# Linear-attention block plus gated MLP on one core: unbroken gate/up groups, other planner priorities, a ring of five exp tiles and two banks for the down projection

## The chip, the core and the metric

The kernel runs on one core of a Trainium2 chip. The metric is device microseconds of one execution; the median of the timed runs counts. The five engines are called here as the profile calls them: PE (matmul; PEld is its weight load), DVE (vector), ACT (scalar), POOL (GpSimd) and SP, whose queue issues nearly all DMAs.

## The reference

With x of 2048 x 448 in bf16, 16 heads of 28, and F = 1792:

```python
xn = layernorm(x); q, k, v = split(xn @ wqkv)          # per head, 28 wide
pq, pk = q @ w_phi, k @ w_phi
phi(z) = concat(softmax(z), softmax(-z))               # 56 features per head
kv = sum_s phi(pk)^T v;  z = sum_s phi(pk)
h = x + ((phi(pq) @ kv) / (phi(pq) @ z + 1e-6)) @ wo
hn = layernorm(h)
out = h + (sigmoid(hn @ w_gate) * (hn @ w_up)) @ w_down
```

## The kernel before

The 2048 tokens are 16 tiles of 128 (t = 0..15) and four chunks of 512 (c = 0..3). The program is a list of operations in `build`, each with an engine, the keys that it reads and writes, an estimated duration `dur`, for a DMA a landing time `lat`, and a priority `prio`. `Graph.schedule` (L69) is a list scheduler that fixes the order on each engine when the kernel is built: it takes the earliest start that any ready operation could have, and among the ready operations of that engine that could start within `TOL` = 0.12 us of it the one with the highest priority. `emit` (L121) writes one in-order stream per engine, with semaphore waits where an operation depends on another engine. So a stream never changes its order on the chip: an operation that the planner put early holds up all that stands behind it. Keys are ordered by program order, so an operation that writes a PSUM bank comes after all operations listed before it that use that bank.

- **Constants and loads** (L307 to L350): POOL sets zeros, the identity, the mask `maskK` and the padded `kvz`. SP issues x tile 0, the k columns of wqkv, x1, the v columns, x2-3, x4-7, then the rest with `after`.
- **wprep** (L365): W_k times w_phi is made on PE (transposes L375, copies on ACT L380 and DVE L383, products L392, copies L398 and L401), with `warm` matmuls on zeros (L356) in the gaps; later the same for W_q.
- **Layernorm 1** (L409 to L442): per tile `bn_stats` and `bn_aggr` on DVE (L416, L418); per group of tiles ([0], [1], [2,3], [4-7], [8-11], [12-15]) `ve1` on DVE (L425), `pow1` on POOL (L427), `nb1` on DVE (L429); then `xn` on ACT (L435) into one of three slots and a DMA transpose on SP into `xnT` (L439).
- **k, v and the kv sum** (L446 to L480): per tile PE makes pk and v (L451); ACT makes exp(pk) and exp(-pk) (L460, L461) and copies v (L463); DVE sums and inverts (L465, L467); POOL multiplies to phi (L469); PE adds to kv (L477) in banks 6 and 7. `ek`, `ss`, `rs`, `phi` and `v1` all have three slots (`NS`).
- **q side** (L482): 16 operations pq (L485) in banks 4 and 5, each with two exps on ACT (L491, L492).
- **Attention per tile** (L549): num on PE (L558; banks 0 and 1 for tiles 1, 3, 5, banks 6 and 7 for the others), six small DVE operations to `rden` (L567 to L578), o on POOL (L580), a transpose, wo on PE in bank 2 (L590), h on DVE (L593), the second layernorm over ACT (L598), DVE and POOL (L603), hn (L607, L608) and a transpose into `xnT` (L611).
- **Gate/up** (L620): chunk 0 in two halves of 256 tokens, then the chunks of 512. The 448 rows of the weights are three k tiles of 128 and one of 64. For two f blocks of 128 columns: operation `gu` (j = 0, banks 4 and 5, priority 20) runs three gate matmuls, three up matmuls (L632) and then `pair`, two matmuls of 64 rows in the two halves of the array (L637, L638). Operations `gg` and `uu` (j = 1, banks 0 and 1, priority 90) begin with their `pair`, then three gate, three up matmuls. ACT makes the sigmoid (L657), DVE the product (L660) into `hhT[c % 2]`.
- **Down** (L664): 14 matmuls per tile (L670) in parts of 4, 4, 3, 3, in bank 3 except for the last chunk; DVE adds h (L676), SP stores (L678).

Of the kernel before, what the change touches and what calls it, by code (L numbers as in the profile page):

```python
# [6 lines left out]
ALU = mybir.AluOpType  # L7
# [7 lines left out]
class _Op:  # L15
    __slots__ = ("i", "eng", "name", "fn", "dur", "prio", "dma", "lat", "deps", "start", "finish", "pos",
                 "need_inc", "sem", "val", "waits", "known", "nkids")


class Graph:  # L20
# [13 lines left out]
    def op(self, eng, name, fn, r=(), w=(), dur=0.1, prio=0.0, dma=None, lat=0.0, nring=0, after=()):  # L34
        o = _Op()
        o.i, o.eng, o.name, o.fn, o.dur, o.prio, o.dma, o.lat = len(self.ops), eng, name, fn, dur, prio, dma, lat
        o.deps = {}
        o.need_inc, o.sem, o.val = False, None, 0
# [30 lines left out]
    def schedule(self):  # L69
        ops = self.ops  # L70
        kids = [[] for _ in ops]
        nd = [len(o.deps) for o in ops]
        for o in ops:
            for j in o.deps:
                kids[j].append(o.i)
        free = {e: 0.0 for e in ENGINES}
        ready = [o.i for o in ops if nd[o.i] == 0]
# [3 lines left out]
        def est(i):  # L81
            o = ops[i]
            a = avail.get(i)
            if a is None:
                a = 0.0
                for j in o.deps:
                    p = ops[j]
                    if p.dma is not None or p.eng != o.eng:
                        f = p.finish + self.SEM_LAT
                    else:  # L90
                        f = p.start + p.dur
                    a = max(a, f)
                avail[i] = a
            return max(a, free[o.eng])
        while ready:
# [10 lines left out]
            o = ops[i]  # L106
            o.start = e
            free[o.eng] = e + o.dur
            o.finish = e + o.dur + o.lat
            ready.remove(i)  # L110
            order.append(i)
            for c in kids[i]:
                nd[c] -= 1
                if nd[c] == 0:
                    ready.append(c)
# [94 lines left out]
P = 128  # L210
D = 448
# [13 lines left out]
def build(nc, A_x, A_wqkv, A_w_phi, A_wo, B_w_gate, B_w_up, B_w_down, out):  # L225
# [10 lines left out]
    with ExitStack() as es:  # L236
# [13 lines left out]
        nb1 = sb("nb1", [P, NT], f32)  # L250
        sum2 = sb("sum2", [P, NT], f32)
# [72 lines left out]
        op("pool", "kvz0", lambda e: e.memset(kvz[:], 0.0), w=["kvz0", "kvz1"], dur=0.9, prio=50)

        def kvz_ones(e):
            for sg in range(2):
                for gg in range(G):
                    p = e.tensor_copy(kvz[:, sg, gg, :].rearrange("p (h e) -> p h e", e=E)[:, :, E - 1], maskK[:, :, 0])
            return p  # L330
        op("pool", "kvzones", kvz_ones, r=["maskK", "kvz0", "kvz1"], w=["kvz0", "kvz1"], dur=1.2, prio=50)


        def xload(a, b, prio, after=()):
            op("sp", "x%d" % a, lambda e: e.dma_start(x_sb[:, a:b, :], x_t[:, a:b, :]), w=[("x", t) for t in range(a, b)],
               dur=0.5, prio=prio, dma="in", lat=1.8 + (b - a) * 0.45, nring=32,
               after=after)

        def wload(j, name, prio, after=()):
            dma_in(wqkv_sb[:, :, j * D:(j + 1) * D], wqkv_v[:, :, j * D:(j + 1) * D], name, 392, prio, after)  # L340
        xload(0, 1, 100)
        wload(1, "wk", 99)
# [5 lines left out]
        xload(1, 2, 97)  # L348
        wload(2, "wv", 96)
        xload(2, 4, 95)  # L350
# [58 lines left out]
        groups = [[0], [1], [2, 3]] + [list(range(4 * c, 4 * c + 4)) for c in range(1, NCH)]  # L409
# [317 lines left out]
```

## Time and profile before

| | |
|---|---|
| median of 3 runs | 237.48 us (236.17 to 238.86) |
| profiled execution | 238.04 us, span 236.3 us |
| PE busy | 218.5 us (92%), 1371 matmuls |
| DVE, ACT, POOL busy | 141.0, 102.3, 60.2 us |
| mean granted PE clock | 0.986 |
| first gate/up matmul, last down matmul's end | 77.25 us, 233.3 us |

The span is from the first to the last instruction of the profiled execution; its own device time is 1.74 us longer. Matmuls overlap in the pipeline, so PE's busy time holds what it waits for within itself; the spacing of starts tells more than a duration. A releaser named "issue" means that the profile shows no wait.

### The profile page before, as it was taken

Reading aid. Unit: us, or ns where it says so; the run is one execution under the profiler, and the core shown is the slowest. Engines: PE = TensorE matmul, PEld = TensorE weight load, DVE = VectorE, ACT = ScalarE, POOL = GpSimd, SP = SyncE. Lnnn points to the kernel's source line nnn. Section 1 sums busy time; section 2 is a strip of 40 time slices with the busy share of each in tenths; the row PEclk is TensorE's granted clock in tenths of the full one; section 3 lists DMA queues with packets and bytes.
Section 4 is the critical chain, followed back from the end, with each engine's and each line's share of the span. In section 5 each row is a group of like instructions: output and inputs, shape, how many; then the busy total and the mean of one; then the engine's idle time right before and its main releaser. Section 6 shows DMA issues by size and latency. Waiting matters only on the chain.

```text
span 236.3 us, 3654 instructions
## 1 busy us (share of the span) xinstructions
PE 218.5 (92%) x1371; PEld 111.1 (47%) x1383; DVE 141.0 (60%) x364; ACT 102.3 (43%) x208; POOL 60.2 (25%) x78
## 2 busy tenths in 40 slices
PE   7679959899997999999999999998999899999994
PEld 3335636555654566665555444333333333334442
DVE  1796995674898687787878676534233243341222
ACT  2588869777689453433343332422312224240000
POOL 7345874874344123203122132000000000000000
PEclk9999988999999799999999999999999999999999
DMA  6697847966123422122122222110000000000101
GB/s 164 171 230 122 251 110 157 239 133 193 22 44 69 89 44 44 27 67 44 22 47 46 65 45 66 22 22 0 21 22 0 19 19 0 3 19 19 58 32 49
DMA packets 35866, 16.66 MB, mean 70 GB/s; under 512 B 27272, under 2 KB 34952, under 8 KB 35848
## 3 DMA queue, kind: packets, MB, share of 16 engines
q1 hardware_dynamic: 35344, 16.39, 29.2%
q8 instruction: 11, 0.18, 0.3%
q10 hardware_dynamic: 504, 0.03, 0.2%
q14 instruction: 7, 0.06, 0.1%
HBM read 8.28 MB, written 1.84 MB: 43 GB/s over the span
## 4 chain that ended last, share of the span: by engine, by line
PE 72%; DVE 10%; DMA 6%; POOL 4%; ACT 4%; issue 2%; SPq 1%; DVEq 0%; POOLq 0%
PE psum L632 33%; PE psum L670 17%; PE psum L637 7%; PE psum L590 5%; POOL phi L469 4%; PE psum L451 3%; PE psum L558 3%; PE psum L485 3%; DMA x_sb<-in_A_x_dram 2%; DMA xnT<-xn_pad 2%; DVE ss L465 2%; DVE hhT L660 1%; DMA xnT<-hn_pad 1%; DVE st L416 1%; PE psum L477 1%
## 5 line engine op out<-in xcount | busy, mean ns | idle before, releaser
L657 ACT ACTIVATE sg_sb<-psum 128x512 bf16<-128x512 f32 (+1 forms) x70 | 35.8, 511 | 83.0 <-PE psum L638 56.7
L660 DVE TENSOR_TENSOR hhT<-psum,sg_sb 128x512 bf16<-128x512 f32 (+1 forms) x70 | 40.4, 584 | 49.5 <-ACT sg_sb L657 31.9
L632 PE MATMUL psum<-xnT,wg_sb 128*128 128x512 bf16 (+1 forms) x202 | 46.8, 338 | 3.1 <-issue 2.4
L632 PE MATMUL psum<-xnT,wu_sb 128*128 128x512 bf16 (+1 forms) x207 | 47.9, 340 | 0.3
L670 PE MATMUL psum<-wd_sb,hhT 128*128 128x448 bf16 x224 | 46.6, 353 | 0.7 <-DVE x_sb L676 0.7
L670 PEld LDWEIGHTS psum<-wd_sb,hhT 128*128 128x128 bf16 x224 | 20.4, 98 | 21.5 <-DVE x_sb L676 2.8
L469 POOL TENSOR_TENSOR phi<-ek,rs 128x896 bf16<-128x896 bf16 x16 | 27.0, 1698 | 10.9 <-DVE rs L467 10.8
L632 PEld LDWEIGHTS psum<-xnT,wu_sb 128*128 128x128 bf16 x210 | 20.7, 99 | 16.0
L632 PEld LDWEIGHTS psum<-xnT,wg_sb 128*128 128x128 bf16 x210 | 16.5, 98 | 24.6 <-issue 11.0
L580 POOL TENSOR_TENSOR o_pad<-c_sb,rden 128x448 bf16<-128x448 bf16 x16 | 15.0, 937 | 47.5 <-DVE rden L578 39.4
L637 PE MATMUL psum<-xnT,wg_sb 64*128 64x512 bf16 (+1 forms) x70 | 20.7, 344 | 1.0 <-DVE hhT L660 0.9
L676 DVE TENSOR_TENSOR x_sb<-psum,x_sb 128x448 bf16<-128x448 f32 x16 | 10.0, 623 | 19.4 <-PE psum L670 19.2
L465 DVE TENSOR_REDUCE ss<-ek 128x32 f32<-128x896 bf16 x16 | 17.2, 1072 | 6.4 <-ACT ek L461 6.4
L638 PE MATMUL psum<-xnT,wu_sb 64*128 64x512 bf16 (+1 forms) x70 | 20.7, 344 | 0.0
L451 PE MATMUL psum<-Wk,xnT 112*128 112x448 bf16 x64 | 15.4, 367 | 2.1 <-DMA xnT<-xn_pad 1.3
L485 PE MATMUL psum<-xnT,Wq 112*112 112x512 bf16 x64 | 15.9, 380 | 0.0
L590 PE MATMUL psum<-wo_sb,oT 112*128 112x448 bf16 x64 | 15.2, 361 | 0.0
L603 POOL TENSOR_TENSOR rst<-ve,neghalf 128x1 f32<-128x1 f32 x16 | 8.8, 553 | 25.0 <-DVE ve L601 24.9
L451 PE MATMUL psum<-wqkv_sb,xnT 112*128 112x448 bf16 x64 | 14.9, 355 | 0.0
L435 ACT ACTIVATE xn_pad<-x_sb,nb,rst 128x448 bf16<-128x448 bf16 x16 | 11.9, 759 | 6.4 <-DVE nb L429 4.4
L598 ACT ACTIVATE junk<-x_sb,nm 128x448 bf16<-128x448 bf16 x16 | 10.6, 664 | 7.5 <-DVE nm L596 7.5
L477 PE MATMUL psum<-v,phi 128*112 128x116 bf16 x128 | 10.0, 223 | 3.7 <-POOL phi L469 3.3
(69 smaller groups left out, 236.2 us busy)
## 6 DMA issues: line engine op xcount, KB each, us to landing
out_dram<-x_sb SPq DMA_DIRECT2D x16, 112.0 KB, 1.7
wd_sb<-in_B_w_down_dram SPq DMA_DIRECT2D x7, 224.0 KB, 4.4
x_sb<-in_A_x_dram SPq DMA_DIRECT2D x3, 448.0 KB, 4.7
wg_sb<-in_B_w_gate_dram SPq DMA_DIRECT2D x3, 448.0 KB, 3.9
wu_sb<-in_B_w_up_dram SPq DMA_DIRECT2D x3, 448.0 KB, 4.5
wqkv_sb<-in_A_wqkv_dram SPq DMA_DIRECT2D x3, 392.0 KB, 4.1
wo_sb<-in_A_wo_dram SPq DMA_DIRECT2D x1, 392.0 KB, 3.6
xnT<-xn_pad SPq DMA_TRANSPOSE x16, 3.3
```

The costliest lines, as they stand in the source:

```text
L451: p = e.matmul(bk(bank)[:, 0:D], lhsT=xnT[t // 4][:GP, kt, TS(t)], rhs=wap(kt), start=(kt == 0), stop=(kt == KT - 1))
L465: op("dve", "ss%d" % t, lambda e: e.tensor_reduce(ss[:, s, :], ek[:, s, :, :].rearrange("p a (h d) -> p (a h) d", d=DH), AX.X, ALU.add), r ...
L469: op("pool", "phi%d" % t, lambda e: e.tensor_tensor(phi[:, s, :, :].rearrange("p a (h d) -> p (a h) d", d=DH), ek[:, s, :, :].rearrange("p ...
L485: p = e.matmul(bk(b)[:GP, 0:512], lhsT=W2[1][:, kt, gg * GP:(gg + 1) * GP], rhs=xnT[c][:GP, kt, :], start=(kt == 0), stop=(kt == KT - 1))
L580: op("pool", "o%d" % t, lambda e: e.tensor_tensor(o_pad[:, s, :, 0:GP].rearrange("p g (h d) -> p g h d", h=4), c_sb[:, s, :, 0:DH].rearran ...
L590: p = e.matmul(bk(2)[:, 0:D], lhsT=oT[:GP, s, kt, :], rhs=wo_sb[:, kt, :], start=(kt == 0), stop=(kt == KT - 1))
L632: p = e.matmul(bk(b)[:, 0:N], lhsT=w[:, kt, fs], rhs=hb[:, kt, ns], start=(st and kt == 0), stop=(sp and kt == 2))
L637: e.matmul(bk(bg)[:, 0:N], lhsT=wg_sb[0:64, 3, fs], rhs=hb[0:64, 3, ns], start=st, stop=not st)
L638: return e.matmul(bk(bu)[:, 0:N], lhsT=wu_sb[64:P, 3, fs], rhs=hb[64:P, 3, ns], start=st, stop=not st, tile_position=(64, 0))
L657: op("act", "sig%d_%d" % (ci, ff), lambda e: e.activation(sg_sb[:, k, 0:N], bk(bg)[:, 0:N], ACT.Sigmoid), r=[B(bg)] + (["sigtab"] if sgn[0 ...
L660: op("dve", "hh%d_%d" % (ci, ff), lambda e: e.tensor_tensor(hhT[(t0 // 4) % NHH][:, ff, ns], bk(bu)[:, 0:N], sg_sb[:, k, 0:N], ALU.mult), ...
L670: p = e.matmul(bk(b)[:, 0:D], lhsT=hhT[c % NHH][:, ff, TS(t)], rhs=wd_sb[:, ff, :], start=(ff == 0), stop=(ff == FT - 1))
```

## The change

`Graph.op` gets `chain` and `urg`. Operations of one chain are ready together, get one start (the latest of each member's need less its offset in the chain) and are emitted back to back; `urg` widens `TOL` for one operation. `gg` and `uu` become members of the chain of their `gu`, at priority 20. `urg` is 0.45 for o, wo and the second layernorm of tiles 0 and 1. Landing times of the first loads and many `dur` values are set anew. The layernorm groups become [0], [1], [2], [3], [4,5], [6,7], [8-11], [12-15], the statistics' priority rises from 46-t to 52-t, and `nb1` moves to POOL, with a new DVE operation `nm1` (minus the mean) ahead of it. `mask0` to `kvzones` stand after the last `pow1` of tiles 6 and 7. `ek` gets five slots inside `hhT[1]`, and `ss`, `rs`, `v1` get five; `phi` keeps three. Down uses banks 2 and 3 in turn for tiles 4 to 11.

```diff
@@ schedule: est of a chain, and the choice
+                a, off = 0.0, 0.0
+                for m in o.chain:
+                    for j in ops[m].deps:
...
+                        a = max(a, f - off)
+                    off += ops[m].dur
...
-                if ops[i].eng == eng0 and e <= m + self.TOL:
+                if ops[i].eng == eng0 and e <= m + self.TOL + ops[i].urg:
...
+            for m in ops[i].chain:
+                o = ops[m]
+                o.start = e
+                e += o.dur
...
+                order.append(m)
@@ buffers
-        ek = sb("ek", [P, NS, 2, D])
-        ss = sb("ss", [P, NS, 2 * H], f32)
-        rs = sb("rs", [P, NS, 2 * H], f32)
+        NE = 5
+        ek = hhT[1][:].rearrange("p f n -> p (f n)")[:, 0:NE * 2 * D].rearrange("p (s a d) -> p s a d", s=NE, a=2)
+        ss = sb("ss", [P, NE, 2 * H], f32)
+        rs = sb("rs", [P, NE, 2 * H], f32)
...
-        v1 = sb("v1", [P, NS, H, EV])
+        v1 = sb("v1", [P, NE, H, EV])
@@ loads: landing times
-        xload(0, 1, 100)
-        wload(1, "wk", 99)
+        xload(0, 1, 100, lat=2.4)
+        wload(1, "wk", 99, lat=4.6)
...
-        xload(1, 2, 97)
-        wload(2, "wv", 96)
-        xload(2, 4, 95)
+        xload(1, 2, 97, lat=4.2)
+        wload(2, "wv", 96, lat=5.4)
+        xload(2, 4, 95, lat=5.5)
...
-                xload(4, 8, 90)
+                xload(4, 8, 90, lat=7.2)
@@ layernorm 1
-        groups = [[0], [1], [2, 3]] + [list(range(4 * c, 4 * c + 4)) for c in range(1, NCH)]
+        groups = [[0], [1], [2], [3], [4, 5], [6, 7]] + [list(range(4 * c, 4 * c + 4)) for c in range(2, NCH)]
...
-               dur=0.58, prio=46 - t)
+               dur=0.57, prio=52 - t)
...
-            op("dve", "nb1_%d" % a, lambda e: e.scalar_tensor_tensor(
-                out=nb1[:, a:b], in0=mv1[:, a:b, 0], scalar=-1.0, in1=rst1[:, a:b], op0=ALU.mult, op1=ALU.mult),
+            op("dve", "nm1_%d" % a, lambda e: e.tensor_scalar(nm1[:, a:b], mv1[:, a:b, 0], -1.0, None, op0=ALU.mult),
+               r=[("mv1", t) for t in ts], w=[("nm1", gi)], dur=0.15, prio=52.9 - a)
+            op("pool", "nb1_%d" % a, lambda e: e.tensor_tensor(nb1[:, a:b], nm1[:, a:b], rst1[:, a:b], ALU.mult),
+               r=[("nm1", gi), ("rst1", gi)], w=[("nb1", gi)], dur=0.25, prio=70 - a)
@@ constants, now listed after layernorm 1
+        op("pool", "mask0", lambda e: e.memset(maskK[:], 1.0), w=["maskK"], dur=0.3, prio=50, after=[pwi[5]])
...
@@ exp of k: slots
-            s = t % NS
+            s = t % NE
+            sp = t % NS
@@ attention: o, wo, h, nm, sq, ve, pow2, hn get urg=ug
+            ug = 0.45 if t < 2 else 0.0
@@ gate/up
-                op("pe", "gu%d_%d" % (ci, ff), fn, r=hk + wgu_keys, w=[B(bg), B(bu)], dur=1.55 * u, prio=20)
+                gch[0] = op("pe", "gu%d_%d" % (ci, ff), fn, r=hk + wgu_keys, w=[B(bg), B(bu)], dur=1.6 * u, prio=20)
...
-                op("pe", "gg%d_%d" % (ci, ff), fn1, r=hk + wgu_keys, w=[B(bg), B(bu)], dur=0.9 * u, prio=90)
-                op("pe", "uu%d_%d" % (ci, ff), fn2, r=hk + wgu_keys, w=[B(bu)], dur=0.65 * u, prio=90)
+                op("pe", "gg%d_%d" % (ci, ff), fn1, r=hk + wgu_keys, w=[B(bg), B(bu)], dur=0.96 * u, prio=20, chain=gch[0])
+                op("pe", "uu%d_%d" % (ci, ff), fn2, r=hk + wgu_keys, w=[B(bu)], dur=0.65 * u, prio=20, chain=gch[0])
@@ down
-                    down(t, 3, [4, 4, 3, 3], 10)
+                    down(t, 3 if t < 4 else (2, 3)[t % 2], [4, 4, 3, 3], 10)
```

## Rows read from the trace of the kernel before

**Rows 1.** Page, granted PE clock in 40 slices of 5.9 us, in tenths

```profile
PEclk9999988999999799999999999999999999999999
```

**Rows 2.** Windows: length, busy us of PE, PEld, DVE, ACT, POOL, clock, DMA, GB/s

```profile
13.30:53.00 39.70, 34.49 (x270) 20.93 (x270) 31.29 (x60) 31.58 (x65) 27.37 (x18) 0.96 0.76 182
...
77.20:211.70 134.50, 131.19 (x783) 61.76 (x795) 77.87 (x213) 44.77 (x95) 16.67 (x23) 0.99 0.15 33
211.70:233.30 21.60, 21.55 (x111) 10.34 (x109) 5.08 (x9) 0.18 (x1) 0.00 (x0) 1.00 0.11 38
```

**Rows 3.** Timeline, start: W_k's preparation (start us, us, engine, line)

```profile
3.90 0.90 POOL L324 MEMSET kvz<- 112x960 bf16 x1
...
7.38 1.09 POOL L329 CAST kvz<-maskK 112x4 bf16<-112x4 f32 x8
...
8.01 0.63 DVE L416 BATCH_NORM_STATS2 st<-x_sb 128x6 f32<-128x448 bf16 x1 [1.16 <-DMA x_sb<-in_A_x_dram]
8.56 0.67 DVE L383 COPY WkT<-psum 112x448 bf16<-112x448 bf16 x2
...
9.28 1.03 PE L392 MATMUL psum<-Wphi,WkT 112*112 112x112 bf16 x16 [1.42 <-DVE WkT L383]
```

**Rows 4.** Timeline, 27 to 35 us: the layernorm of tiles 8 to 11

```profile
27.06 0.12 DVE L418 BATCH_NORM_AGGREGATE mv<-st 128x2 f32<-128x6 f32 x1
...
28.99 1.70 POOL L469 TENSOR_TENSOR phi<-ek,rs 128x896 bf16<-128x896 bf16 x1
...
29.05 1.65 DVE L429 SCALAR_TENSOR_TENSOR nb<-mv,rst 128x4 f32<-128x4 f32 x1
...
30.74 2.06 ACT L435 ACTIVATE xn_pad<-x_sb,nb,rst 128x448 bf16<-128x448 bf16 x3 [1.76 <-DVE nb L429]
...
34.11 1.70 PE L451 MATMUL psum<-Wk,xnT 112*128 112x448 bf16 x4
```

**Rows 5.** Windows around the two stretches at the lower clock

```profile
33.60:37.10 3.50, 3.40 (x19) 2.21 (x20) 2.23 (x8) 2.47 (x6) 2.00 (x2) 0.56 0.49 100
29.70:33.70 4.00, 1.32 (x19) 0.98 (x17) 3.93 (x9) 2.90 (x5) 3.49 (x3) 0.95 0.37 112
75.30:77.20 1.90, 0.07 (x2) 0.00 (x0) 1.90 (x7) 1.88 (x5) 1.44 (x3) 1.00 0.16 31
...
77.60:81.00 3.40, 3.40 (x18) 1.71 (x16) 1.97 (x6) 1.52 (x3) 0.94 (x1) 0.51 0.42 86
```

**Rows 6.** Timeline, before the first gate/up matmul

```profile
76.43 0.62 ACT L492 ACTIVATE eq<-psum 112x512 bf16<-112x512 f32 x1
...
77.25 0.49 PE L632 MATMUL psum<-xnT,wg_sb 128*128 128x256 bf16 x3 [1.88 <-issue]
```

**Rows 7.** PE's timeline: pairs alone and pairs joined

```profile
110.00 0.38 PE L558 MATMUL psum<-kvz,eq 112*128 112x120 bf16 x4
110.21 0.49 PE L632 MATMUL psum<-xnT,wg_sb 128*128 128x256 bf16 x3
...
113.45 0.37 PE L558 MATMUL psum<-kvz,eq 112*128 112x120 bf16 x4
113.76 0.39 PE L637 MATMUL psum<-xnT,wg_sb 64*128 64x512 bf16 x1
...
114.08 0.82 PE L632 MATMUL psum<-xnT,wg_sb 128*128 128x512 bf16 x3
...
209.89 0.39 PE L637 MATMUL psum<-xnT,wg_sb 64*128 64x512 bf16 x1
...
210.12 0.38 PE L637 MATMUL psum<-xnT,wg_sb 64*128 64x512 bf16 x1
```

**Rows 8.** PE's waits, 59 to 234 us: total us, times, longest

```profile
PE psum L637 <- DVE hhT L660: 0.9, 1, 0.9
PE psum L670 <- DVE x_sb L676: 0.7, 1, 0.7
PE psum L632 <- DVE hhT L660: 0.7, 3, 0.3
```

More of the change, by code (lines that the diff above doesn't have):

```diff
@@ L16 @@
     __slots__ = ("i", "eng", "name", "fn", "dur", "prio", "dma", "lat", "deps", "start", "finish", "pos",
-                 "need_inc", "sem", "val", "waits", "known", "nkids")
+                 "need_inc", "sem", "val", "waits", "known", "chain", "head", "urg")
 class Graph:
@@ L32, in __init__, with op @@
         self.ring = {}
-    def op(self, eng, name, fn, r=(), w=(), dur=0.1, prio=0.0, dma=None, lat=0.0, nring=0, after=()):
+    def op(self, eng, name, fn, r=(), w=(), dur=0.1, prio=0.0, dma=None, lat=0.0, nring=0, after=(), chain=None, urg=0.0):
         o = _Op()
@@ L37, in op @@
         o.deps = {}
+        o.chain, o.head, o.urg = [o.i], o.i, urg
+        if chain is not None:
+            o.head = self.ops[chain].head
+            self.ops[o.head].chain.append(o.i)
         o.need_inc, o.sem, o.val = False, None, 0
@@ L71, in schedule @@
         kids = [[] for _ in ops]
-        nd = [len(o.deps) for o in ops]
+        nd = [0] * len(ops)
         for o in ops:
             for j in o.deps:
-                kids[j].append(o.i)
+                if ops[j].head != o.head:
+                    nd[o.head] += 1
+                    kids[j].append(o.head)
         free = {e: 0.0 for e in ENGINES}
-        ready = [o.i for o in ops if nd[o.i] == 0]
+        ready = [o.i for o in ops if o.head == o.i and nd[o.i] == 0]
         order = []
@@ L84, in est @@
             if a is None:
[L85 to L92, printed above, removed]
+                a, off = 0.0, 0.0
+                for m in o.chain:
+                    for j in ops[m].deps:
+                        p = ops[j]
+                        if p.head == o.head:
+                            continue
+                        if p.dma is not None or p.eng != o.eng:
+                            f = p.finish + self.SEM_LAT
+                        else:
+                            f = p.start + p.dur
+                        a = max(a, f - off)
+                    off += ops[m].dur
                 avail[i] = a
@@ L105, in schedule @@
             _, e, i = best
[L106 to L109, printed above, removed]
             ready.remove(i)
[L111 to L115, printed above, removed]
+            for m in ops[i].chain:
+                o = ops[m]
+                o.start = e
+                e += o.dur
+                free[o.eng] = e
+                o.finish = e + o.lat
+                order.append(m)
+                for c in kids[m]:
+                    nd[c] -= 1
+                    if nd[c] == 0:
+                        ready.append(c)
         assert len(order) == len(ops)
@@ L250, in build @@
         nb1 = sb("nb1", [P, NT], f32)
+        nm1 = sb("nm1", [P, NT], f32)
         sum2 = sb("sum2", [P, NT], f32)
@@ L324, in build, with xload @@
[L324 to L334, printed above, removed]
+        def xload(a, b, prio, after=(), lat=None):
@@ L487, in mm @@
                 return p
-            op("pe", "pq%d_%d" % (c, gg), mm, r=W2q + [("xnT", 4 * c + i) for i in range(4)], w=[B(b)], dur=0.9, prio=prio)
+            op("pe", "pq%d_%d" % (c, gg), mm, r=W2q + [("xnT", 4 * c + i) for i in range(4)], w=[B(b)], dur=0.87, prio=prio)
             def eqf(e):
@@ L509, in build, with kvz_ones @@
                 xi[t] = xnorm(t)
+        op("pool", "mask0", lambda e: e.memset(maskK[:], 1.0), w=["maskK"], dur=0.3, prio=50, after=[pwi[5]])
+        op("pool", "mask1", lambda e: e.affine_select(out=maskK[:], in_=maskK[:], compare_op=ALU.is_ge, fill=0.0, base=0,
+                                                      channel_multiplier=1, pattern=[[-DH, 4], [0, EV]]),
+           r=["maskK"], w=["maskK"], dur=0.35, prio=50)
+        op("pool", "mask2", lambda e: e.affine_select(out=maskK[:], in_=maskK[:], compare_op=ALU.is_ge, fill=0.0,
+                                                      base=DH - 1, channel_multiplier=-1, pattern=[[DH, 4], [0, EV]]),
+           r=["maskK"], w=["maskK"], dur=0.35, prio=50)
+        op("pool", "kvz0", lambda e: e.memset(kvz[:], 0.0), w=["kvz0", "kvz1"], dur=0.9, prio=50)
+        def kvz_ones(e):
+            for sg in range(2):
+                for gg in range(G):
+                    p = e.tensor_copy(kvz[:, sg, gg, :].rearrange("p (h e) -> p h e", e=E)[:, :, E - 1], maskK[:, :, 0])
+            return p
+        op("pool", "kvzones", kvz_ones, r=["maskK", "kvz0", "kvz1"], w=["kvz0", "kvz1"], dur=1.2, prio=50)
         for t in range(NT):
```

62 lines of the change are left out of this document (28 added, 34 removed).

## The prediction

> **What bounds the kernel now.** I read the page first, then the windows, then the timeline where they show holes.
>
> The page gives PE 218.5 us busy of a span of 236.3, so PE is the engine to count. Its clock is full but for two places [rows 1]. The windows split the span [rows 2]. From the first gate/up matmul (77.2) to the last down matmul (233.3) PE is busy 131.19 of 134.50 and 21.55 of 21.60 us: there only PE's own work, its clock and 3.3 us of gaps count. From 13.3 to 53.0, which is from the first exp of k to the last, no engine is full: PE 34.49 of 39.70 (pipelined time, so less in truth), ACT 31.58, DVE 31.29, POOL 27.37. That stage is bound by waits in fixed streams, and its fullest engine other than PE, ACT, has 8.1 us to spare.
>
> Where are the waits? At the start DVE copies WkT at 8.56, behind the statistics of tile 2, which waited 1.16 us for x; PE's products of W_k follow at 9.28 after 1.42 us idle [rows 3]. In the middle, DVE aggregates tile 11 only at 27.06; nb1 of tiles 8 to 11 starts at 29.05 and takes 1.65 us; ACT's xn waits 1.76 us for it and starts at 30.74; the next pk matmuls start at 34.11 [rows 4]. PE is busy 1.32 of the 4.00 us from 29.7 to 33.7, and in the 3.5 us after that it has a mean clock of 0.56, so mostly the lower of its levels, 1.2 instead of 2.4 GHz [rows 5]. Before the first gate/up matmul PE stands idle for 1.88 us [rows 6], and then again runs 3.4 us at 0.51 [rows 5].
>
> In gate/up the cost that the change aims at can be seen in the starts of the pairs [rows 7]. A pair alone that ends a stretch (113.76, next matmul 114.08) takes 0.32 us; a pair followed by a pair (209.89, then 210.12) takes 0.23. That is 0.09 us for leaving the 64-row form. Entering it costs as much again: num's four matmuls at 113.45 are followed by the pair 0.31 us later, while the four at 110.00 are followed by a full-row matmul in 0.21. So each separate stretch of pairs costs some 0.19 us. Of the 35 groups of two f blocks, 21 have their two pairs joined (the last at 209.89), 14 have them apart: gg, at priority 90, ran ahead of gu, or other work came between.
>
> **The change, part by part**, against the profiled execution of 238.04 us.
>
> *Early part.* (a) With the new landing times the planner expects x2-3 late, as it is, and can place the WkT copies ahead of its statistics. They end at 9.23; without the wait of 1.16 and the 0.63 of the statistics they would end some 1.8 us earlier [rows 3]. Gain 0 to 1.8. Next late would be the copies of W2 on ACT and DVE. (b) Statistics at 52-t come before ss and rs of earlier tiles, so tiles 8 to 11 are normalised as soon as their group is complete. The hole is worth 4.00 - 1.32 = 2.7 us of idle PE, plus half of the time at the lower clock, 3.5 x 0.44 = 1.5: 4.2 at most [rows 5]. (c) nb1 on POOL takes DVE's 1.65 us off the path, but nm1 is a new DVE operation of the same small size, six becoming eight groups; no row shows it. Bounds per group: 0.15, which the other small DVE operations take, and 1.65, as nb1 did when phi (28.99, 1.70 us) ran on POOL beside it [rows 4]. I take 0.15, because nm1 needs nothing from POOL and can run while pow1 does. (d) Five exp slots let ACT run two tiles further ahead of phi; without a row that shows ACT held for long, I count this only as what lets (a) and (b) go through. (e) The constants go behind pow1 of tiles 6 and 7: kvz's two steps are 0.90 + 1.09 = 2.0 us of POOL [rows 3], and their priority of 50 puts them ahead of phi. Before, phi had not begun then; now they stand in its stream. Cost 0, if POOL's 39.70 - 27.37 = 12.3 us of slack [rows 2] takes them, to 2.0.
>
> Sum of the gains 1.8 + 4.2 = 6.0. It is limited by ACT's 8.1 us of slack, which no in-order stream uses up; I take half, 3.0, because (c) and (e) pull against it and because PE fills part of the time won by doing num and wo of later tiles less early, which it must then do later. Bounds: -1.5 (both late groups held 1.65 in nm1 and nothing won, PE taking up half) to +6.0.
>
> *Hand-over to gate/up.* `urg` lets the planner keep DVE or PE free up to 0.45 us for tiles 0 and 1. But the first gu also uses bank 4 or 5, which all 16 pq use ahead of it: the last exp of these ended at 76.43 + 0.62 = 77.05, and PE began at 77.25 [rows 6]. So landing the tiles earlier wins nothing unless ACT too is earlier. I take 0 by itself, bounds -1.0 to +1.9 (the idle time), and leave the stretch at half clock where it is, since the same idle time comes before it; if that goes, 3.4 x 0.49 = 1.7 more [rows 5].
>
> *Unbroken groups.* 14 stretches of pairs fewer at 0.19: 2.7 us, on PE's path, nothing beside it. Bounds 2.0 (some starts still held by a bank) to 2.7.
>
> *Stalls in gate/up and down.* PE waited 0.9 us once in front of a lone pair for a product on DVE, and 0.7 in three more such waits; 0.7 once for the last add of a down tile in the single bank [rows 8]. The second bank takes away the last; joined groups alternate their banks evenly and should take the 0.9, but the shorter groups of 256 columns leave DVE and ACT less time for the two products. I take 1.2, bounds 0 to 2.3. Moving gg from priority 90 to 20 also means that num and wo (60-t, 70-t) go first whenever they are ready between groups; they wait behind a whole group when not.
>
> The end (last add and store, 3.0 us after 233.3) stays. Sum: 3.0 + 0 + 2.7 + 1.2 = 6.9, so 238.04 - 6.9 = 231.1. The median shown is 0.56 below the profiled execution, so **230.6 us**.
>
> A page speaks against (c). The Trainium skill, "SBUF — State Buffer", section "Who interferes with whom", says that VectorE and GpSimd share a pair of SBUF ports under an exclusive lock, and that `tensor_scalar`, which nm1 is, may use it. By that rule nm1 would be held as nb1 was; the 1650 ns of nb1, ending within 10 ns of the phi beside it, agree with a lock of that kind. What this would make of the time is the second rival.
>
> **The rivals.**
> 1. *All of it is won.* The early 6.0, both clock dips away (1.7 for the second), 2.7, and 2.3 of stalls: 12.7, so 225.3, less 0.56: 224.8 us. For it: 8.1 us of slack on ACT, and PE busy only 1.32 of 4.00 in the hole. Against it: pq's exps must all be done before gate/up, and ACT has those too.
> 2. *The early gain is given back at POOL and DVE.* nm1 held by phi in both late groups costs 3.3, the constants 2.0, which together eat 5.3 of 6.0; PE keeps 2.7 + 1.2 and some half us: 238.04 - 4.4 - 0.56 = 233.1. For it: the 1.65 of nb1. Against it: nm1 stands directly behind ve1 in program order and a hold there would overlap ve1's.
> 3. *Hardly anything:* early part -1.5, joins 2.0, stalls 0: 237.0.
> 4. *Slower: attention starves behind the groups.* A PE step was at most a half group, two times three matmuls of up to 0.82 and a pair of 0.32, 1.96 us; it is now a whole one, 3.9. A num or wo that just misses waits on average 1 us longer. With three such steps per tile (two nums, wo) and 8 tiles in the chunks with 512 columns, that is 24 us if none of it is hidden. The point from which it decides: 6.9 + 2.4 = 9.3 us unhidden. At half, 12 us, the time is 238.04 - 6.9 + 12 - 0.56 = 242.6. For it: banks 6 and 7 hold one tile's num at a time. Against it: PE's 3.3 us idle in 134.5 [rows 2] show that gate/up and down work was there almost always, and down can fill in.
>
> **How the numbers follow.** Forecast (228.5 to 232.5) 0.45; rival 1 (below 228.5) 0.22; rival 2 (to 235) 0.17; rival 3 0.09; rival 4 0.07. One per cent, 2.4 us, is about what a measurement of this kernel can tell from no change. Faster than 235.1: 0.45 + 0.22 + 0.16 = 0.83; slower than 239.9: 0.06; between: 0.11. The range takes rivals 1 and 2 whole: 224.8 rounds to 224.5, and 236.0 lies past rival 2 by a part of rival 3.
>
> **What would show it.** Right: 35 stretches of pairs, each with two pairs some 0.23 us apart; no PE hole with a half clock behind it near 30 us; the first gate/up matmul at about 74; no PE wait on the add of down. Wrong: nm1 with more than 1 us, ACT's xn waiting for POOL's nb1, phi delayed by L324 and L329, a first gate/up matmul still at 77, or PE idle for several us ahead of chunk 1, 2 or 3 with hn's transposes landing just before.

## The result, and the profile after

The median of the kernel after is 228.65 us (4 runs, 227.87 to 230.17), beside 237.67 us (236.17 to 238.86) of four runs of the kernel before. The ratio is 0.9631, 95% interval 0.9557 to 0.9706: 9.0 us faster. The forecast was 230.6 us, 6.9 us below the median of 237.48 us that was known then.

The profiled execution took 227.87 us with a span of 226.2. Differences below between two medians are differences of their ratios to the kernel before, times 237.67 us; stages are read from the profiled executions. One run of a_pairs_apart (the profiled one, 240.27 us at a mean granted clock of 0.943) and one of a_sigld (229.66 us) were over 1.5% longer than the fastest of their kernel and are left out of the medians and ratios.

The page of the kernel after: busy time of the engines, and the granted clock in 40 slices.

```profile
PE 212.0 (94%) x1372; PEld 109.7 (48%) x1383; DVE 143.3 (63%) x368; ACT 101.7 (45%) x208; POOL 62.3 (28%) x88
...
PEclk9999999999999999999999999999999999999999
```

Neither dip of [rows 1] is there. That is this one execution: the other three show a mean clock of 0.991 to 0.993, so in them some stretch still ran at the lower level. No trace shows where.

The windows of the kernel after (length, busy us of PE, PEld, DVE, ACT, POOL, clock, DMA share, GB/s), for the stages of [rows 2] and three pieces of the early part:

```profile
12.00:48.00 36.00, 33.34 (x276) 20.68 (x275) 32.64 (x66) 31.32 (x64) 31.30 (x35) 1.00 0.95 206
...
22.00:28.00 6.00, 6.00 (x55) 3.77 (x52) 5.79 (x13) 6.00 (x13) 4.91 (x4) 1.00 1.10 189
28.00:34.00 6.00, 5.33 (x40) 3.17 (x40) 5.83 (x11) 5.30 (x12) 5.66 (x5) 1.00 1.11 332
34.00:40.00 6.00, 6.00 (x62) 4.25 (x61) 5.22 (x10) 5.65 (x13) 6.00 (x5) 1.00 1.03 217
...
72.17:223.08 150.91, 148.12 (x895) 72.26 (x903) 86.30 (x227) 45.74 (x97) 17.13 (x24) 1.00 0.15 35
```

For comparison, the last of these windows in the kernel before, from its first gate/up matmul to its last down matmul:

```profile
77.25:233.25 156.00, 152.74 (x893) 72.06 (x904) 82.88 (x220) 44.91 (x95) 16.67 (x23) 0.99 0.14 33
```

So 5.1 us went ahead of the first gate/up matmul (77.25 to 72.17) and another 5.1 behind it (156.0 to 150.9). The hole of [rows 5] is closed. In the stage that bounds the early part POOL is now busy 31.30, ACT 31.32, DVE 32.64 and PE 33.34 of 36.0 us; before, POOL was busy 27.37 of 39.70 us [rows 2]. Almost all of the 5.1 us behind the first gate/up matmul is PE's busy time (152.74 to 148.12), not its idle time (3.3 to 2.8).

The timeline of the kernel after, cut to the steps that the prediction names (start us, us, engine, line; in brackets the wait ahead of it and what ended it):

```profile
3.13 0.90 POOL L518 MEMSET kvz<- 112x960 bf16 x1
...
7.40 0.38 DVE L381 COPY WkT<-psum 112x448 bf16<-112x448 bf16 x1
...
8.70 1.00 PE L390 MATMUL psum<-Wphi,WkT 112*112 112x112 bf16 x16 [0.89 <-DMA Wphi<-in_A_w_phi_dram]
...
16.87 1.08 POOL L523 CAST kvz<-maskK 112x4 bf16<-112x4 f32 x8
...
18.45 1.70 POOL L469 TENSOR_TENSOR phi<-hhT,rs 128x896 bf16<-128x896 bf16 x1 [0.51 <-DVE rs L467]
...
19.10 1.07 DVE L423 TENSOR_SCALAR ve<-mv 128x4 f32<-128x4 f32 x1
...
20.09 0.15 DVE L427 TENSOR_SCALAR nm<-mv 128x4 f32<-128x4 f32 x1
...
20.25 1.01 POOL L425 TENSOR_TENSOR rst<-ve,neghalf 128x4 f32<-128x4 f32 x1
...
22.92 0.78 ACT L434 ACTIVATE xn_pad<-x_sb,nb,rst 128x448 bf16<-128x448 bf16 x1
...
28.54 1.07 DVE L423 TENSOR_SCALAR ve<-mv 128x4 f32<-128x4 f32 x1
...
32.78 14.94 POOL L469 TENSOR_TENSOR phi<-hhT,rs 128x896 bf16<-128x896 bf16 x9
...
72.17 0.49 PE L651 MATMUL psum<-xnT,wg_sb 128*128 128x256 bf16 x3
...
73.23 0.67 ACT L616 ACTIVATE junk<-x_sb,nm 128x448 bf16<-128x448 bf16 x1 [2.80 <-DVE nm L614]
...
74.01 1.28 ACT L676 ACT_TABLE_LOAD   x1
...
74.01 0.28 PE L656 MATMUL psum<-xnT,wg_sb 64*128 64x256 bf16 x1 [0.80 <-DVE den L593]
...
76.20 0.50 PE L651 MATMUL psum<-xnT,wg_sb 128*128 128x256 bf16 x3 [1.15 <-DVE hhT L679]
...
125.97 0.39 PE L656 MATMUL psum<-xnT,wg_sb 64*128 64x512 bf16 x1
126.19 0.38 PE L656 MATMUL psum<-xnT,wg_sb 64*128 64x512 bf16 x1
126.51 0.82 PE L651 MATMUL psum<-xnT,wg_sb 128*128 128x512 bf16 x3
```

Tile 8 is normalised at 22.92 where it was 30.74 [rows 4]. The pair at 126.19 follows 0.22 us behind the first, and the next full-row matmul 0.32 behind the second: one stretch of two pairs. 34 of the 35 groups look so, against 21 before. The one that doesn't is the first: its second pair waits 0.80 us for bank 0, which den of tile 5 still reads.

All waits of PE for a semaphore in the last window, after (total us, times, longest), beside [rows 8]:

```profile
PE psum L651 <- DVE hhT L679: 1.4, 2, 1.1
PE psum L656 <- DVE den L593: 0.8, 1, 0.8
```

The wait on down's add is gone, and the two longest waits now stand in the first group. The 1.1 ends with a product that came late because ACT loaded its table (1.28 us at 74.01) before the first sigmoid. The load itself came late because ACT's stream has an activation of the second layernorm ahead of it, which had waited 2.80 us for DVE (73.23). In the kernel before the same load ran right behind the last exp, 0.2 us ahead of the first gate/up matmul (77.25):

```profile
77.06 1.28 ACT L657 ACT_TABLE_LOAD   x1
```

### The profile page after: what moved, and what is told of

Same layout as the page of the kernel before. It is cut to its first block, busy times and chain, and to the rows that moved or that the text cites. A ratio compares the mean times of both kernels' runs of the same rounds, so it can differ in the third digit from the quotient of the medians.

```text
span 226.2 us, 3686 instructions
## 1 busy us (share of the span) xinstructions
PE 212.0 (94%) x1372; PEld 109.7 (48%) x1383; DVE 143.3 (63%) x368; ACT 101.7 (45%) x208; POOL 62.3 (28%) x88
## 4 chain that ended last, share of the span: by engine, by line
PE 73%; DVE 9%; ACT 7%; DMA 6%; POOL 2%; issue 1%; ACTq 1%; SPq 0%; DVEq 0%; POOLq 0%
PE psum L651 32%; PE psum L689 18%; PE psum L656 7%; DMA xnT<-xn_pad 6%; PE psum L450 5%; PE psum L608 5%; PE psum L485 3%; PE psum L576 2%; DVE hn_pad L625 2%; DVE hhT L679 1%; PE psum L477 1%; DVE ss L465 1%; ACT xn_pad L434 1%; ACT hhT L460 1%; ACT hhT L461 1%
## 5 line engine op out<-in xcount | busy, mean ns | idle before, releaser
L651 PE MATMUL psum<-xnT,wu_sb 128*128 128x512 bf16 (+1 forms) x207 | 47.3, 336 | 0.3
L689 PEld LDWEIGHTS psum<-wd_sb,hhT 128*128 128x128 bf16 x224 | 21.5, 98 | 19.9 <-DVE x_sb L695 0.4
L651 PEld LDWEIGHTS psum<-xnT,wg_sb 128*128 128x128 bf16 x210 | 17.0, 97 | 23.4 <-issue 11.6
L469 POOL TENSOR_TENSOR phi<-hhT,rs 128x896 bf16<-128x896 bf16 x16 | 26.8, 1697 | 2.8 <-DVE rs L467 2.6
L695 DVE TENSOR_TENSOR x_sb<-psum,x_sb 128x448 bf16<-128x448 f32 x16 | 9.9, 621 | 20.4 <-PE psum L689 20.3
L656 PE MATMUL psum<-xnT,wg_sb 64*128 64x512 bf16 (+1 forms) x70 | 18.3, 339 | 0.8 <-DVE den L593 0.8
L465 DVE TENSOR_REDUCE ss<-hhT 128x32 f32<-128x896 bf16 x16 | 16.9, 1056 | 2.4 <-ACT hhT L461 2.3
L657 PE MATMUL psum<-xnT,wu_sb 64*128 64x512 bf16 (+1 forms) x70 | 18.3, 339 | 0.0
L450 PE MATMUL psum<-Wk,xnT 112*128 112x448 bf16 x64 | 14.6, 352 | 2.5 <-DMA xnT<-xn_pad 2.5
L611 DVE SCALAR_TENSOR_TENSOR x_sb<-psum,x_sb 128x448 bf16<-128x448 f32 x16 | 10.0, 623 | 5.8 <-PE psum L608 5.6
```

Source lines behind the costliest of these rows:

```text
L450: p = e.matmul(bk(bank)[:, 0:D], lhsT=xnT[t // 4][:GP, kt, TS(t)], rhs=wap(kt), start=(kt == 0), stop=(kt == KT - 1))
L465: op("dve", "ss%d" % t, lambda e: e.tensor_reduce(ss[:, s, :], ek[:, s, :, :].rearrange("p a (h d) -> p (a h) d", d=DH), AX.X, ALU.add), r ...
L469: op("pool", "phi%d" % t, lambda e: e.tensor_tensor(phi[:, sp, :, :].rearrange("p a (h d) -> p (a h) d", d=DH), ek[:, s, :, :].rearrange(" ...
L651: p = e.matmul(bk(b)[:, 0:N], lhsT=w[:, kt, fs], rhs=hb[:, kt, ns], start=(st and kt == 0), stop=(sp and kt == 2))
L656: e.matmul(bk(bg)[:, 0:N], lhsT=wg_sb[0:64, 3, fs], rhs=hb[0:64, 3, ns], start=st, stop=not st)
L657: return e.matmul(bk(bu)[:, 0:N], lhsT=wu_sb[64:P, 3, fs], rhs=hb[64:P, 3, ns], start=st, stop=not st, tile_position=(64, 0))
```

## The experiments

Twelve kernels were run. The stages of their profiled executions, with "kv end" the end of the last kv matmul, "first gu" the start of the first gate/up matmul, "main" the time from there to the end of the last down matmul, and "joined" the groups with one stretch of two pairs:

| kernel | kv end | first gu | main | joined | median, us |
|---|---|---|---|---|---|
| before | 56.9 | 77.25 | 156.0 | 21 | 237.67 |
| after | 51.1 | 72.17 | 150.9 | 34 | 228.65 |
| a_no_chain | 51.2 | 72.59 | 156.4 | 20 | 233.62 |
| b_chain | 58.7 | 79.03 | 151.6 | 35 | 235.27 |
| a_pairs_apart | | | | 0 | 235.60 |
| a_bank3 | 51.3 | 72.12 | 155.7 | 34 | 231.97 |
| a_stats46 | 58.6 | 79.44 | 151.0 | 34 | 235.36 |
| a_ring3 | 55.4 | 76.72 | 150.9 | 34 | 232.24 |
| a_nb1_dve | 52.8 | 73.52 | 151.2 | 34 | 230.23 |
| a_lat_old | 54.2 | 75.27 | 150.9 | 34 | 229.96 |
| b_stats52 | 55.6 | 75.91 | 156.0 | 21 | 236.19 |
| a_sigld | 50.5 | 71.55 | 149.6 | 34 | 227.49 |
| a_sigld_nbank | 51.9 | 71.24 | 149.6 | 35 | 225.63 |
| a_xn5_sigld | 52.0 | 72.81 | 149.8 | 34 | 227.28 |

Names with a_ are the kernel after with the edit shown, those with b_ the kernel before. Line numbers in rows of an experiment may differ from those of the kernel after by a few.

### The unbroken groups: taken out, put in alone, and their price by itself

**a_no_chain**, from after:

```diff
-... gg: dur=0.96 * u, prio=20, chain=gch[0])
-... uu: dur=0.65 * u, prio=20, chain=gch[0])
+... gg: dur=0.96 * u, prio=90)
+... uu: dur=0.65 * u, prio=90)
```

> The changed kernel with gg and uu taken out of the chain and back at priority 90. Theory (separate stretches of pairs cost 0.19 us each on PE): the number of joined groups falls from 34 back towards 21, so 13 x 0.19 = 2.5 us come back, and up to 1 us of waits for products: 231.0 to 232.2 us, the first gate/up matmul still within 0.5 us of 72.2. Rival (the order of gate/up does not matter, the early part is everything): within 0.6 us of 228.65.

Measured: 233.62 us, ratio 0.9826 (0.9788 to 0.9864), 4.6 us behind after. 20 groups stay joined. That is more than 14 joins at the predicted 0.19 (2.7 us), and above the expected range. Its last window:

```profile
72.59:228.95 156.36, 153.13 (x905) 72.11 (x903) 85.79 (x226) 44.55 (x96) 17.25 (x24) 0.99 0.16 34
```

PE's idle time is 3.2 us, as before and nearly as after (2.8); the busy time is 5.0 longer, part of it at a lower clock (mean 0.99; this execution has such a stretch around its first gate/up matmul, that of after has none).

**b_chain**, from before, with the scheduler that can chain:

```diff
-                op("pe", "gu%d_%d" % (ci, ff), fn, ...
+                gch[0] = op("pe", "gu%d_%d" % (ci, ff), fn, ...
-... gg, uu: prio=90)
+... gg, uu: prio=20, chain=gch[0])
```

> The kernel before with nothing but the chain of gu, gg and uu at priority 20. Theory: 35 groups joined, 14 x 0.19 = 2.7 us less and up to 1 us of waits less, first gate/up matmul near 77: 234.0 to 235.0 us. Rival (attention starves behind whole groups): PE idle for several us ahead of a chunk, 237.7 us or more.

Measured: 235.27 us, ratio 0.9878 (0.9825 to 0.9931), 2.9 us faster than before. Its last window:

```profile
79.03:230.65 151.62, 149.22 (x904) 71.77 (x904) 83.82 (x220) 45.12 (x95) 16.61 (x23) 1.00 0.15 34
```

The window is 4.4 us shorter than that of before, and PE idles 2.4 us in it: num and wo lose nothing by waiting for whole groups. Not all of the 4.4 us is joins: the window of before holds the stretch at the lower clock behind the first gate/up matmul [rows 5], and that of b_chain holds none. And the planner made another early part as well, whose kv sum ends 1.8 us later, so that the median keeps less.

**a_pairs_apart**, from after: all 35 groups get one stretch of pairs more, and nothing else changes; the order of operations is the same.

```diff
 def fn1 (gg)
-                    pair(e, True)
-                    return full(e, wg_sb, bg, False, True)
+                    full(e, wg_sb, bg, True, False)
+                    ... the two matmuls of 64 rows: gate with stop=True, up with start=True
```

> The changed kernel with the pair of gg moved behind its three gate matmuls, so that in each of the 35 groups the two pairs stand apart; the same matmuls, and the streams of the other four engines stay as they are. Theory (a separate stretch of pairs costs 0.19 us on PE): 35 x 0.19 = 6.6 us more, 234.3 to 235.6 us, all of it between the first gate/up and the last down matmul (150.9 to about 157.5 us). Rival (the 0.19 us is pipeline time that is hidden, and the chain gained by its order): under 2 us more.

Measured: 235.60 us, ratio 0.9889 (0.9847 to 0.9931), 6.1 us behind after. By 35 stretches that is 0.175 us each; the two intervals together leave some 2.0 us either way, so 0.12 to 0.23. The 0.19 of the prediction is within it. The starts in its trace, at a granted clock of 0.95, say the same:

```profile
129.91 0.84 PE L651 MATMUL psum<-xnT,wg_sb 128*128 128x512 bf16 x3
130.59 0.84 PE L651 MATMUL psum<-xnT,wu_sb 128*128 128x512 bf16 x3
131.36 0.39 PE L656 MATMUL psum<-xnT,wg_sb 64*128 64x512 bf16 x1
...
131.68 0.84 PE L651 MATMUL psum<-xnT,wg_sb 128*128 128x512 bf16 x3
```

Three full-row matmuls take 0.68 us ahead of other full-row matmuls and 0.77 ahead of a pair; the pair alone takes 0.32, against 0.22 for a pair that a pair follows in the kernel after. That is 0.09 for entering the 64-row form and 0.10 for leaving it.

### Two banks for down

**a_bank3**, from after:

```diff
-                    down(t, 3 if t < 4 else (2, 3)[t % 2], [4, 4, 3, 3], 10)
+                    down(t, 3, [4, 4, 3, 3], 10)
```

> The changed kernel with down in bank 3 alone for all tiles before the last chunk. Theory (PE waits for the add of a finished tile before it can open the bank again): one to three waits of 0.7 us come back, 229.3 to 230.8 us. Rival (a whole gate/up group always fits in between): within 0.4 us of 228.65.

Measured: 231.97 us, ratio 0.9751 (0.9719 to 0.9783), 2.9 us behind after: more than both theories said. PE's waits from 50 us on:

```profile
PE psum L651 <- DVE hhT L679: 1.7, 3, 1.1
...
PE psum L689 <- DVE x_sb L695: 1.4, 2, 0.7
PE psum L689 <- DVE ve L619: 0.7, 1, 0.7
```

In the new order three down matmuls wait, 0.7 us each, 2.1 in all, two of them for the add of the tile before (the third is put down to `ve`, another operation on DVE); before it was one [rows 8]. The whole groups bring this, not the rest of the change: b_chain, which also has one bank, shows the same three waits:

```profile
PE psum L683 <- DVE x_sb L689: 1.4, 2, 0.7
PE psum L683 <- DVE nm L608: 0.7, 1, 0.7
```

I read it as down tiles that stand closer together, because whole groups leave the planner fewer places for them; why they do was not tested. (The last window is 4.7 us longer, but it has a stretch at the lower clock, which the profiled execution of after lacks; so the waits and the medians are the better measure.)

### The early part

**a_stats46**, from after:

```diff
-... bst, agg: prio=52 - t)     ve1: prio=53 - a)     nm1: prio=52.9 - a)
+... bst, agg: prio=46 - t)     ve1: prio=47 - a)     nm1: prio=46.9 - a)
```

> The changed kernel with the statistics' priorities of layernorm 1 back at 46-t (and 47-a, 46.9-a for the small ones). Theory (late statistics of tiles 8 to 11 made the hole near 30 us): xn of tile 8 falls back from 22.9 to about 27 or later, PE has a hole of 2 to 4 us, perhaps with the lower clock behind it, and the time rises by 2.5 to 4.5 us to 231.2 to 233.2. Rival (the finer groups, the true landing times and the ring carry the early gain by themselves): within 0.8 us of 228.65.

Measured: 235.36 us, ratio 0.9903 (0.987 to 0.9936), 6.5 us behind after. Windows and timeline at the same place as those of after above:

```profile
22.00:28.00 6.00, 3.56 (x23) 1.99 (x22) 3.99 (x8) 3.24 (x7) 4.01 (x3) 0.91 0.81 185
28.00:34.00 6.00, 5.72 (x51) 3.88 (x48) 3.38 (x7) 3.56 (x8) 3.28 (x4) 0.81 0.42 126
34.00:40.00 6.00, 3.64 (x23) 2.18 (x24) 3.68 (x13) 3.60 (x6) 4.14 (x4) 0.76 0.46 107
```

```profile
33.77 0.76 ACT L434 ACTIVATE xn_pad<-x_sb,nb,rst 128x448 bf16<-128x448 bf16 x1
```

The hole is back and deeper than before: tile 8 is normalised at 33.77, PE is busy 12.9 of these 18.0 us at 0.76 to 0.91 of the clock (15.2 of the same 18.0 in the kernel before), and DVE, ACT and POOL are busy 3.2 to 4.1 of each 6.0 us. All of the loss, which is more than expected, lies ahead of the first gate/up matmul (79.44); main is as after.

**b_stats52**, from before:

```diff
-... bst, agg: prio=46 - t)     ve1, nb1: prio=47 - a)
+... bst, agg: prio=52 - t)     ve1, nb1: prio=53 - a)
```

> The kernel before with nothing but the statistics' priorities of layernorm 1 raised to 52-t (and 53-a). Theory (the late statistics of tiles 8 to 11 made the hole near 30 us by themselves): the hole and the lower clock behind it go, kv ends 2 to 4 us before 56.9, 233.5 to 235.5 us. Rival (with three exp slots and groups of four tiles the early part cannot use it; the parts only work together): kv ends within 1 us of 56.9 or later, 236.7 us or more.

Measured: 236.19 us, ratio 0.9916 (0.9881 to 0.9952), 2.0 us faster than before, with kv end 1.3 us earlier. Near 30 us the hole and the lower clock behind it are gone (PE is busy 4.00 of the 4.00 us from 29.7 to 33.7), but this profiled execution ran at the lower clock from 11 to 19 us, which takes part of its kv end. The priority that costs 6.5 us when taken away gives only 2.0 when it comes alone.

**a_ring3**, from after:

```diff
-        NE = 5
+        NE = 3
```

> The changed kernel with three exp slots instead of five. Theory (the ring is what lets ACT and PE run ahead while POOL does phi without a break from 33 to 48 us): ACT waits for phi, the end of kv moves from 51.1 to 52.5 to 54 us, and the time rises by 1.5 to 3 us to 230 to 231.7. Rival (three slots were enough, as no long wait of ACT for phi stood in the trace of before): within 0.6 us of 228.65.

Measured: 232.24 us, ratio 0.9771 (0.9738 to 0.9804), 3.3 us behind after and somewhat more than expected; kv end 55.4, with a stretch at the lower clock from 38 to 42 us in it. The edit takes `ss`, `rs` and `v1` to three slots too. One wait of PE, one window and one row of ACT:

```profile
PE psum L450 <- ACT hhT L461: 2.8, 3, 1.8
```

```profile
34.00:40.00 6.00, 4.05 (x30) 2.51 (x28) 3.61 (x6) 4.66 (x11) 3.60 (x4) 0.83 0.86 199
```

```profile
35.06 0.76 ACT L434 ACTIVATE xn_pad<-x_sb,nb,rst 128x448 bf16<-128x448 bf16 x1 [2.29 <-DMA xnT<-xn_pad]
```

PE's wait of 1.8 us is for exps that stand in ACT's stream behind this xn, and the xn waits 2.29 us for a transpose to free its slot. No wait of ACT for phi shows in the trace. So what three slots cost is measured, and that they cost it in the early part (main is 150.9); that exps held by phi are the cause is not shown. With three slots the planner also makes another order. With five, POOL runs nine phi without a break (32.78 for 14.94 us in the timeline of after).

**a_nb1_dve**, from after:

```diff
-            op("dve", "nm1_%d" % a, ...)
-            op("pool", "nb1_%d" % a, ...)
+            op("dve", "nb1_%d" % a, lambda e: e.scalar_tensor_tensor(... mv1, -1.0, rst1 ...), prio=53 - a)
```

> The changed kernel with nb1 on DVE again, as one operation behind pow1, without nm1. Theory (nb1 on DVE can be held by phi on POOL and holds what stands behind it on DVE): one or two nb1 of 1 us or more, the end of kv 0.5 to 2 us later, 229.0 to 231 us. Rival (nm1 with ve1 and pow1 cost DVE and POOL as much): within 0.6 us of 228.65.

Measured: 230.23 us, ratio 0.9678 (0.9641 to 0.9714), 1.1 us behind after, but the intervals overlap: unclear. The two last nb1 of its timeline:

```profile
21.56 1.17 DVE L427 SCALAR_TENSOR_TENSOR nb<-mv,rst 128x4 f32<-128x4 f32 x1
...
32.27 0.93 DVE L427 SCALAR_TENSOR_TENSOR nb<-mv,rst 128x4 f32<-128x4 f32 x1
```

On DVE nb1 of the two late groups is held for 1.17 and 0.93 us, when it comes at the time of a phi, and ends within 0.02 us of that phi (21.02 and 31.49 us, 1.70 each); kv end is 1.7 later.

**a_lat_old**, from after: the landing times of the kernel before.

```diff
-               lat=lat or 1.8 + kb / 200.0, ...
+               lat=lat or 1.8 + kb / 250.0, ...
-        xload(0, 1, 100, lat=2.4) ...
+        xload(0, 1, 100) ...
```

> The changed kernel with the old landing times of the loads. Theory (the planner then places the statistics of x2-3 ahead of the copies of WkT, as before): the first pk matmul moves from 11.1 to about 12 us, and half to all of that reaches the end: 229.0 to 230.0 us. Rival (the start is held by the loads and transposes anyway): within 0.5 us of 228.65.

Measured: 229.96 us, ratio 0.9672 (0.9639 to 0.9704), 1.0 us behind after with overlapping intervals: unclear. Its first pk matmul comes at 12.63 instead of 11.09 and its kv end 3.1 later; its profiled execution (231.03 us) was the longest of its four and ran at the lower clock from 39 to 43 us, so the trace shows more than the median.

### The first group, and a better version

**a_sigld**, from after: the sigmoid's table is loaded by a tiny activation ahead of gate/up, and every sigmoid reads that key.

```diff
+        op("act", "sigld", lambda e: e.activation(sgw[:], zero[:, 0:2], ACT.Sigmoid),
+           r=["zero"], w=["exptab", "sigtab"], dur=1.45, prio=100)
```

> The changed kernel with one tiny sigmoid on ACT as soon as the last exp of q is done, so that its table is loaded there and not at the first gate/up block. Theory (PE's 1.1 us wait for a product at the start of gate/up is the table load of 1.28 us): that wait goes, 0.7 to 1.2 us less on PE, and where the lower clock came with the idle time there, up to 1.7 us more: 226.5 to 228.0 us. Rival (the wait is then for den of tile 5 or the next transposes anyway): within 0.5 us of 228.65.

Measured: 227.49 us, ratio 0.9567 (0.9512 to 0.9623), 1.5 us ahead of after; the two intervals overlap, so the median alone is unclear, but the trace shows the step. Timeline:

```profile
69.89 1.28 ACT L636 ACT_TABLE_LOAD   x1
...
71.55 0.49 PE L654 MATMUL psum<-xnT,wg_sb 128*128 128x256 bf16 x3
...
73.28 0.36 ACT L679 ACTIVATE sg_sb<-psum 128x256 bf16<-128x256 f32 x1
```

The table comes at 69.89, while ACT has nothing else to do, and PE's wait of 1.1 for the first product shrinks to 0.3. The wait for den of tile 5 (0.8) stays.

**a_sigld_nbank**, with the same edit and tile 5's num in the other banks:

```diff
-            return (0, 1) if t in (1, 3, 5) else (6, 7)
+            return (0, 1) if t in (1, 3) else (6, 7)
```

> As a_sigld, and num of tile 5 in banks 6 and 7 instead of 0 and 1, which the first gg needs. Theory (gg waits 0.8 us for den of tile 5): another 0.3 to 0.8 us less, 226.0 to 227.6 us. Rival (tile 5 then waits for the banks of tile 4, and attention comes later by about as much): equal to a_sigld or up to 1 us slower.

Measured: 225.63 us (224.72 to 225.97), ratio 0.9489 (0.9446 to 0.9533): 3.4 us ahead of after with intervals that don't touch. It beats both kernels. PE's longest waits from 50 us on:

```profile
PE psum L577 <- DVE b_sb L589: 0.8, 1, 0.8
PE psum L577 <- DVE den L594: 0.5, 1, 0.5
...
PE psum L654 <- issue: 0.3, 2, 0.2
```

No gate/up matmul waits for den any more, and all 35 groups are joined. The longest waits left are those of num for its bank. Part of the 3.4 us may be clock: the mean granted clock is 1.0 in four of its six runs and 0.998 in a fifth, and 1.0 in one of four of after. What the bank gives alone is unclear: the interval overlaps that of a_sigld, the two profiled executions, both at clock 1.0, are 0.25 us apart (225.93 and 225.68), and main is 149.6 in both.

**a_xn5_sigld**, a_sigld with five slots for the padded xn:

```diff
-        xn_pad = sb("xn_pad", [P, NS, KT, P])
+        NX = 5
+        xn_pad = sb("xn_pad", [P, NX, KT, P])
```

> As a_sigld, and five slots instead of three for the normalised tiles that wait for their transposes. Theory (in the changed kernel ACT waits 2.5 us and PE 2.9 us in the early part for transposes, because xn may run only three tiles ahead): kv ends 0.5 to 2 us before 51.1, and 0.5 to 1.5 us less than a_sigld: 225.2 to 227.3 us. Rival (the transposes themselves are the limit, 4.1 us from issue to landing beside the loads): kv ends within 0.4 us of 51.1, the time equal to a_sigld.

Measured: 227.28 us, ratio 0.9565 (0.9521 to 0.9608), the same as a_sigld; kv end 52.0, not earlier than 50.5. PE's wait for the transposes in the early part:

```profile
PE psum L452 <- DMA xnT<-xn_pad: 3.6, 6, 0.9
```

With five slots ACT no longer waits for one (2.1 us in a_sigld), and PE still waits for the transposes (2.5 us in a_sigld). Slots are not what holds them; the transposes take 4.4 us to landing in the median, against 3.9 in a_sigld.

## Why the prediction was right, and which terms were not

**The early part ("I take half, 3.0") was mis-sized: 5.1 us.** (a) The WkT copies end at 7.78 instead of 9.23, but the gain stops at the next thing that is late, the DMA of w_phi, for which the products wait 0.89 us, and not the copies of W2 that the prediction named; they begin 0.6 earlier and the first pk matmul 0.9. (b) The hole and the half clock behind it are gone, as the 4.2 at most of the prediction had it. The kv sum ends 5.8 us earlier: 0.9 from the start, 4.9 from the middle, so a little more than the hole itself, and neither (c) nor (e) took any of it back; 0.75 went at the hand-over. Halving it by ACT's slack was too careful: ACT stayed with 4.7 of 36.0 us idle, and POOL with as little, so the streams came nearer to full than I had allowed. (d) was counted as "what lets (a) and (b) go through", and that is its kind: 3.3 us by a_ring3. The parts do not add up: 6.5 (statistics), 3.3 (ring), 1.1 (nb1) and 1.0 (landing times) make 11.9, more than twice the gain, and the first two, which alone are clear of the noise, make 9.8; statistics alone on the kernel before give 2.0. So the statistics pay in full only together with the rest.

**nm1 and rival 2.** nm1 took 0.15, as assumed, and for the reason given against rival 2: a hold fell on ve1 in front of it. ve1 of tiles 8 to 11 ran from 19.10 for 1.07 us and ended 0.02 us after the phi that had begun at 18.45; nm1 came directly behind, at 20.09, ahead of pow1 (20.25) and not beside it as (c) had it. ve1 of tiles 12 to 15 was held alike (28.54, 1.07). The exclusive lock that the Trainium skill describes ("SBUF — State Buffer", "Who interferes with whom") agrees with that end. The hold of ve1 cost little here, since pow1, which needs it, runs on POOL behind the same phi. On DVE, nb1 was held 1.17 and 0.93 (a_nb1_dve). (e) The constants cost nothing that shows: kvz's memset went into POOL's idle start (3.13), and only the mask and the casts stand shortly before the first phi, at 16.87 for 1.08; phi then waits 0.51 for rs, not for them. One sign of being wrong did show, in small: ACT's xn waits for POOL's nb1, 1.6 us in all at tiles 1 and 2; in the kernel before it waited 4.4 us for DVE's.

**The hand-over ("0 by itself").** From kv end to the first gate/up matmul it was 20.3 us and is now 21.1: a loss of 0.75, inside the bounds. `urg` was not tried alone, nor were the constants at their old place.

**Unbroken groups (2.7) were right in mechanism and size for the joins.** 13 more groups are joined; at the measured 0.175 that is 2.3 us. Of the 5.1 us behind the first gate/up matmul that leaves 2.8: up to 1.7 for the clock (below), 0.5 less idle time of PE, and 0.6 without a name. Taking the chains out costs 4.6 us in the median, 2.2 more than its 14 joins; the two intervals together leave 2.0 us either way, so whether the new order of PE's work is worth anything beyond the joins stays open. The clock alone does not make the difference: at 0.999 a_no_chain took 232.78 us, at 1.0 after took 227.87.

**Stalls (1.2): the sum failed in its parts.** The old waits of [rows 8], 2.3 us, went, but 1.4 + 0.8 new ones came, so that PE's waits for a semaphore are 0.1 shorter. I had put down the loss of the second bank as 0.7, from the order of before; in the new order it is 2.9 (a_bank3). And the new waits are in the first group, a place that the prediction did not look at. Whole groups alone do not bring them: b_chain loads the table at 78.84, ahead of its first gate/up matmul at 79.03, and waits neither for den nor for a product in its first group. Nor does the rest of the change alone: a_no_chain loads the table at 70.54 and does not wait for den. In the kernel after, with both, den of tile 5 comes at 73.78, 1.6 us behind the first gate/up matmul, and the table load stands behind an activation of the second layernorm. Which term besides the chains made that order (`urg` or another) is not shown.

**The clock behind the first gate/up matmul** was left in place. The profiled execution shows none of it, which gives up to 1.7 us of the 5.1 in the last window; the other runs' mean clocks say that in them some remained. That may be one reason why the profiled execution gained 10.2 us and the median 9.0. It can also cost nothing: a_ring3 has such a stretch from 75 to 79 us, through its first group, and its main is 150.9 all the same, presumably because PE would have waited there for den (that wait is gone).

**The rivals.** Rival 4 (starvation) falls: PE idles 2.8 of 150.9 us, 2.4 of 151.6 in b_chain. Rival 2 falls with ve1 above; rival 3 with the 5.1. Rival 1, all of it won, came nearer than it was given credit for on the early part, and not on the stalls.

## What to carry to other kernels

In a program of fixed in-order streams, priorities, landing times and buffer counts work together: price them by taking one out of the finished version, and do not add such prices up. A suspected cost per switch is best measured by doubling its count with everything else in place (35 stretches more, 6.1 us). After a change that makes steps longer, read the first step of the next stage row by row: a bank handed over late and a table load there were worth 3.4 us together, part of it perhaps clock.

## What the hardware showed that was not expected

- The table load of 1.28 us before the first sigmoid stood on PE's path, and cost nothing that shows when it was asked for 1.7 us ahead of the first gate/up matmul (a_sigld).
- Runs of one kernel differ in their mean granted clock: 1.0, 0.992, 0.993 and 0.991 in the four runs of the kernel after, with 227.87, 228.56, 230.17 and 228.74 us. The clock alone does not set their order.
- The transposes of xn took longer from issue to landing: median 3.3 us before, 4.1 after, and PE waits 2.9 us for them in the early part. That the part is denser does not explain it: in a_stats46, where the hole is back, they take 4.2. The cause is open. The page's DMA line of the kernel after (issues, median us to landing):

```profile
xnT<-xn_pad SPq DMA_TRANSPOSE x16, 4.1
```
